# Sliding-window attention and a Sinkhorn-routed mixture of experts on one core: batch 7's blocks of x turned on TensorE, and four loads and starts moved

## The chip, the core and the metric

The kernel runs on one core of a Trainium2 chip. A core has a matrix engine (TensorE, PE in the profile), a vector engine (DVE), a scalar engine (ACT), GpSimd (POOL) and SyncE (SP), which here only issues transfers. Sixteen DMA engines carry the transfers of all queues. The time is that of one execution on the device, in microseconds (us); smaller is better. Three runs before the change gave a median of 1063.09 us (1062.86 to 1065.08).

## The reference

The inputs are q, k and v of 8 batches, 8 heads, 576 rows and 64 columns, and the weights of 8 experts. Attention sees at most 128 rows back and carries a bias that falls linearly with distance; its output, as 4608 rows of 512, is x. Every row then goes through every expert, and the experts' results are added with weights that come from eight rounds of normalising over rows and over columns.

```python
scores = where(0 <= rel < 128, q @ k.T / 8 - slope[h] * abs(rel), -1e9)
x = (softmax(scores) @ v).transpose(0, 2, 1, 3).reshape(4608, 512)
P = exp(x @ w_gate - max)
for _ in range(8):
    P /= P.sum(1, keepdims=True) + 1e-9
    P /= P.sum(0, keepdims=True) + 1e-9
    P *= 4608 / 8
for e in range(8):
    out += P[:, e:e+1] * (relu(x @ w1[e]) @ w2[e])
```

## The kernel before, in words

The order of the work is written out by hand: every engine carries out its instructions in the order in which the Python code emits them, and waits on semaphores where data or a buffer is not there yet. Tiles come from pools with a fixed number of buffers, so a load into a tile waits until the tile's previous user is done.

There are three stages.

**Attention, with experts 0 and 1 as filling.** A loop over `steps` runs through 8 batches, 5 blocks of rows (`kb`, four of 128 rows and a tail of 64) and 2 halves of the heads (`u`); inside a batch the half-blocks are numbered `at = 2 * kb + u`, 0 to 9. A half-block is a chain: scores on PE (L372, L379), exponentials on ACT (L390), a mask product on DVE (L403), the product with v on PE (`values`, L426), a reciprocal and a scaling on DVE (L436, L437). The result `xsb`, one block of x with rows in partitions, must be turned before the experts can use it (`turn_x`, L444). Batches below `XPE = 3` are turned on PE, with four transposes into PSUM (L454) and a copy by DVE (L462); the later batches are turned by a DMA that SP issues (L464). The turned x stays in `xT`. The four tails of 64 rows share blocks 32 to 35 in pairs, and the last of these, block 35, holds the tails of batches 6 and 7.

Between the parts of that chain the class `Filler` puts pieces of the first two experts on PE: `l1` is x times w1 (L102), `l2` is the second product (L115). A piece is allowed when its blocks of x are done (`filler.ready`) and its expert is in `filler.allowed`. Expert 0 is allowed from the start, expert 1 after half-block 1 of batch 1. Results go to a scratch tensor in HBM (`ysp`) by stores that SP issues (L484), those of the first four blocks of expert 0 in one store (L673). `gates` (L467, L470) multiplies the turned blocks by the gate weights; after the loop `gates(4 * B - 4, NBLK)` does blocks 28 to 35 in one go.

**Sinkhorn.** DVE does the eight rounds, with small products on PE, and `filler` puts batch 7's blocks of experts 0 and 1 between them.

**Experts 2 to 7.** Two thirds of the time; PE runs L829 and L884 without a break.

Two queues matter for the change. SP issues, in this order, the loads of batch 0 (L288, L334, L223), then q and k of batch 1 (`load_qk(1)`, L232), the tails of q and k of batch 1 (`load_tail(1)`, L223), the first block of v of batch 1 (`load_v(NKB)`, L334), and from the loop two more blocks of v, q and k of batch 2 after half-block 3 of batch 0, then v again. POOL casts each block of v to half precision (`cast_v`, L344) and issues the loads of the experts' weights, which convert to half precision on the way (`load_weights`, L86 and L88). It takes these in order too: the load of expert 1 stands behind the cast of v's block 0 of batch 1 (emitted after half-block 1 of batch 0).

Of the kernel before, what the change touches and what calls it, by code (L numbers as in the profile page):

```python
# [14 lines left out]
def kernel(  # L15
# [15 lines left out]
    B, H, S, Dh = q.shape  # L31
# [10 lines left out]
    NKB = 5  # L42
# [101 lines left out]
    XPE, YO = 3, 6  # L144
# [58 lines left out]
    if True:  # L203
# [16 lines left out]
        def load_tail(b):  # L220
            t32 = asb.tile([P, H, Dh], FP32, name=f"t32_{b}", tag="s32", bufs=5)
            for lo, src in ((0, q), (TL, k)):
                nc.sync.dma_start(  # L223
                    out=t32[lo : lo + TL], in_=src[b, :, SM:S, :].rearrange("h s d -> s h d")
                )
            tails[b] = t32

        def load_qk(b):
            q32 = per.tile([P, H, RI * Dh], FP32, name=f"q32_{b}", tag="a8", bufs=8)
            k32 = per.tile([P, H, RI * Dh], FP32, name=f"k32_{b}", tag="a8", bufs=8)  # L230
            for t, src in ((q32, q), (k32, k)):
                nc.sync.dma_start(  # L232
                    out=t, in_=src[b, :, 0:SM, :].rearrange("h (p i) d -> p h (i d)", i=RI)
                )
            raw[b] = (q32, k32)

        def cast_qk(b, j):

            if j == 0:
                c16s[b] = per.tile([P, 2, RI, H, Dh], FP16, name=f"c16_{b}", tag="a8", bufs=8)  # L240
            for n in (1, 0):
                src = raw[b][n][:, 2 * j : 2 * j + 2, :].rearrange("p h (i d) -> p i h d", i=RI)
                to = c16s[b][:, n, :, 2 * j : 2 * j + 2, :]
                if n == 0:
                    nc.vector.tensor_copy(out=to, in_=src)
                else:
                    nc.scalar.copy(out=to, in_=src)
            if j == NDT - 1:
                raw.pop(b)
# [80 lines left out]
        def load_v(m):  # L330
            b, kb = divmod(m, NKB)
            v32 = asb.tile([P, H, Dh], FP32, name=f"v32_{b}_{kb}", tag="s32", bufs=5)
            nk = P if kb < NKB - 1 else TL
            nc.sync.dma_start(  # L334
                out=v32[0:nk],
                in_=v[b, :, P * kb : P * kb + nk, :].rearrange("h s d -> s h d"),
            )
            v32s[b, kb] = v32

        def cast_v(m):  # L340
            b, kb = divmod(m, NKB)
            vt = asb.tile([P, H, Dh + 2], FP16, name=f"v_{b}_{kb}", tag="v", bufs=6)
            nk = P if kb < NKB - 1 else TL
            nc.gpsimd.tensor_copy(out=vt[0:nk, :, 0:Dh], in_=v32s.pop((b, kb))[0:nk])  # L344
            nc.gpsimd.memset(vt[:, :, Dh : Dh + 2], 1.0)
            vs[b, kb] = vt
# [7 lines left out]
        def sizes(kb):  # L354
            nk = P if kb < NKB - 1 else TL
            nn = 0 if kb == NKB - 1 else (P if kb < NKB - 2 else TL)
            return nk, nn
# [51 lines left out]
        def values(b, kb, u):  # L409
# [31 lines left out]
                op=ALU.mult,  # L441
            )

        def turn_x(b, kb):  # L444
            nk, _ = sizes(kb)
            if kb < NKB - 1:
                to = xT[:, 4 * b + kb]
            else:
                to = xT[:, 4 * B + b // 2, :, TL * (b % 2) : TL * (b % 2) + TL]
            xsb = xsbs.pop((b, kb))  # L450
            if b < XPE:
                ps = aps.tile([P, NDT, P], FP16, name=f"psX_{b}_{kb}", tag="pmm", bufs=4)
                for j in range(NDT):
                    nc.tensor.matmul(  # L454
                        out=ps[:, j, 0:nk],
                        lhsT=xsb[0:nk, 2 * j : 2 * j + 2, :],
                        rhs=ident[0:nk, 0:nk],
                        is_transpose=True,
                        start=(j == 0),
                        stop=(j == NDT - 1),  # L460
                    )
                nc.vector.tensor_copy(out=to, in_=ps[:, :, 0:nk])  # L462
            else:
                nc.sync.dma_start(out=to, in_=xsb[0:nk].rearrange("p h d -> p (h d)"), transpose=True)  # L464
# [36 lines left out]
        for n in range(2, len(spans)):  # L501
            order += [(0, n), (1, n - 2)]
        order += [(1, len(spans) - 2), (1, len(spans) - 1)]
        filler = Filler(
            (e, *spans[n], lambda e=e, n=n: unit_atoms(e, *spans[n], aps, ("pmm", "pmm"), (4, 4), keep))
            for e, n in order
        )
# [93 lines left out]
        nc.gpsimd.dma_start(out=wg_sb, in_=moe_w_gate.rearrange("(dt p) e -> p dt e", p=P))  # L601
        cast_v(3)
        cast_v(4)
        load_qk(1)
        load_tail(1)
        load_v(NKB)


        steps = [(b, kb, u) for b in range(B) for kb in range(NKB) for u in range(2)]
# [14 lines left out]
        for n, (b, kb, u) in enumerate(steps):  # L624
            nxt = steps[n + 1] if n + 1 < len(steps) else None
            at = 2 * kb + u
            left = ((8 if b < XPE else 10) - at) % 10 + 1
            budget = filler.backlog() / (11 if (b, at) == (XPE, 0) else left)
            if nxt:
                if nxt[0] < XPE and nxt[1:] == (RI - 2, 1):  # L630
                    turn_pe(nxt[0], 0, NDT)
                if nxt == (1, 0, 0):
                    cast_qk(1, 0)
                    cast_qk(1, 1)
                    for j in range(NDT):
                        turn_pe(1, 1, j)
                        turn_pe(1, 0, j)
                        if j < 2:
                            cast_qk(1, j + 2)
                        filler.fill(1.0)  # L640
                if n == 0:
                    scores(*nxt)
                elif nxt[2] == 0:
                    scores(*nxt)
                    scores(*nxt[:2], 1)
                exps(*nxt)
            got = filler.fill(1.0)
            if nxt:
                masks(*nxt)
            values(b, kb, u)  # L650
            if n > 0 and u == 0 and steps[n - 1][0] < XPE:
                turn_x(*steps[n - 1][:2])
            if u == 1 and n // 2 + NKB < B * NKB:
                cast_v(n // 2 + NKB)
            filler.fill(budget - got)
            if at == 0 and b > XPE:
                filler.ready = 4 * b
            if at < 8 and b < XPE:
                filler.ready = 4 * b + at // 2
            if at == 8 and b < XPE:  # L660
                filler.ready = 4 * b + 4
            if b >= XPE and u == 1:
                turn_x(b, kb)
            if u == 1:
                if kb == 1 and b > 0:
                    gates(4 * b - 4, 4 * b)
                if n // 2 + NKB + 1 < B * NKB:
                    load_v(n // 2 + NKB + 1)
            if b == 0 and at == 1:
                load_weights(1)  # L670
            if b == 1 and at == 1:
                filler.allowed.add(1)
                nc.sync.dma_start(out=ysp[0, 0:RI].rearrange("m p d -> p m d"), in_=first_y[0])  # L673
            if (b, at) == (0, 3):
                load_qk(2)
            if (b, at) == (0, 7):
                homes(1)
            if (b, at) == (1, 3):
                homes(2)
            if b == 1 and 3 <= at <= 6:  # L680
                cast_qk(2, at - 3)
            if b == 1 and 4 <= at <= 7:
                turn_pe(2, 1, at - 4)
                turn_pe(2, 0, at - 4)
            if 1 <= b < B - 2 and at == 3:
                load_qk(b + 2)
            if 1 <= b < B - 2 and at >= 8:
                cast_qk(b + 2, at - 8)
            if 2 <= b < B - 1:
                if at < 2:  # L690
                    cast_qk(b + 1, at + 2)
                if at == 1:
                    turn_qk(b + 1)
                    order_qk(b + 1, 1, range(NDT))
                if at == 5:
                    turn_tail(b + 1)
                if at in (6, 7):
                    order_qk(b + 1, 0, range(2 * at - 12, 2 * at - 10))
            if b < B - 1 and at == (1 if b > 1 else 5) and b:
                load_tail(b + 1)  # L700
            if 10 * b + at >= 66:
                i = 10 * b + at - 66
                if i % 8 == 0:
                    home_last(2 + i // 8)
                (load_w2 if i % 8 < 4 else load_w1)(2 + i // 8, i % 4, 4)
            if (b, at) == (7, 0):
                todo += sums_of(2, *extras(2))
            if b == 7 and at >= 5:
                some(1)
# [9 lines left out]
        F1_6 = lp.tile([P, NF2, HB], FP16, name="f1_6")  # L719
        todo += sums_of(4, *extras(4))  # L720

        filler.fill(4.4)
        gates(4 * B - 4, NBLK)
        filler.ready = NBLK

# [316 lines left out]
```

## Time and profile before

| | |
|---|---|
| median of three runs | 1063.09 us |
| the profiled execution | 1062.15 us |
| its span, first to last instruction | 1060.4 us |
| PE busy | 1031.0 us, 97% of the span |
| DVE, ACT, POOL busy | 629.8, 433.9 and 76.9 us |
| end of attention, start of L829 | about 284 us and 348 us |

The span is what the views of the profile cover; 1.75 us of the profiled execution lie around it. A line of a timeline gives the start and the length in us, the engine, the line of the kernel, the operation, what it writes and reads, and in square brackets how long the engine was idle before it and what ended the idle time. "L102 x8" are eight matmuls in one line. Busy tenths stand in 40 slices of 26.5 us.

### The profile page before, as it was taken

The page shows a single profiled execution, that of the slowest core. Times are in us where ns is not written, and L with a number is a line of the kernel's source. Part 1 is how long each engine was busy: PE and PEld are TensorE (multiplying, and loading weights), DVE is VectorE, ACT ScalarE, POOL GpSimd, SP SyncE. Part 2 cuts the span into 40 slices and gives each one's busy share as a digit, 9 for nine tenths or more (in the row PEclk, how much of TensorE's full clock was granted, in tenths as well). Part 3 has the DMA queues.
Part 4 walks back from the last instruction along what each step waited for, and adds up shares of the span by engine and source line. Part 5 has one row for each costly group of instructions (what it writes and reads, how often), then busy time and mean ns, then how long its engine had stood idle before and what let it go on. Part 6 is the DMA issues. An engine that isn't in the chain of part 4 may idle for free.

```text
span 1060.4 us, 21106 instructions
## 1 busy us (share of the span) xinstructions
PE 1031.0 (97%) x8986; PEld 802.0 (76%) x8986; DVE 629.8 (59%) x1166; ACT 433.9 (41%) x729; POOL 76.9 (7%) x139
## 2 busy tenths in 40 slices
PE   6799999999899999999999999999999999999998
PEld 4565444444444888888888888888888888888887
DVE  4565665555488565655655655655655655555555
ACT  6565554555233333333333333333333333333332
POOL 2122032334000000000000000000000000000000
PEclk9999999999999999999999999999999999999999
DMA  9996598969992501201211211211220220220240
GB/s 227 250 221 165 103 213 206 195 156 167 193 202 72 120 21 50 71 24 48 70 28 43 70 41 31 70 24 48 71 63 8 71 68 4 70 70 2 71 90 20
DMA packets 168574, 99.14 MB, mean 94 GB/s; under 512 B 87424, under 2 KB 159904, under 8 KB 168480
## 3 DMA queue, kind: packets, MB, share of 16 engines
q1 hardware_dynamic: 153744, 79.80, 29.9%
q0 software_dynamic: 14304, 17.84, 10.3%
q8 instruction: 70, 1.15, 0.4%
q14 instruction: 24, 0.20, 0.1%
q10 hardware_dynamic: 432, 0.16, 0.1%
HBM read 87.74 MB, written 19.02 MB: 101 GB/s over the span
## 4 chain that ended last, share of the span: by engine, by line
PE 90%; DMA 6%; DVE 1%; SPq 1%; ACT 1%; issue 0%; POOL 0%; DVEq 0%
PE psh L829 35%; PE psS_m L884 31%; PE psh L102 11%; PE psy L115 10%; DMA xT<-xsb 2%; DMA v<-in_v_dram 2%; PE psN L426 1%; DMA w1t<-in_moe_w_dram 1%; PE psS L372 1%; SPq L223 1%; DMA pbc<-ptd 1%; DVE yo L496 1%; SPq L334 0%; PE psy L949 0%; DMA k<-in_k_dram 0%
## 5 line engine op out<-in xcount | busy, mean ns | idle before, releaser
L836 ACT ACTIVATE hs<-psh 128x512 f16<-128x512 f32 x432 | 257.9, 597 | 453.4 <-PE psh L829 372.6
L829 PE MATMUL psh<-aux,w1l 128*128 128x256 f16 x2880 | 372.6, 273 | 0.4 <-DVE aux L813 0.4
L829 PEld LDWEIGHTS <-w1l 128*128 128x128 f16 x2880 | 281.7, 98 | 33.5 <-issue 0.6
L884 PEld LDWEIGHTS <-hs 128*128 128x128 f16 x2568 | 251.2, 98 | 29.1
L841 DVE TENSOR_TENSOR hs<-hs 128x1024 f16<-128x1024 f16 x107 | 74.0, 691 | 274.5 <-ACT hs L836 274.5
L884 PE MATMUL psS_m<-w2l,hs 128*128 128x256 f16 x1440 | 186.6, 273 | 0.0
L102 PE MATMUL psh<-xT,w1t 128*128 128x512 f16 (+1 forms) x640 | 144.1, 364 | 7.9 <-DMA w1t<-in_moe_w_dram 3.0
L115 PE MATMUL psy<-w2t,hT 128*128 128x512 f16 x576 | 133.8, 379 | 2.3 <-DMA w2t<-in_moe_w_dram 1.6
L813 DVE TENSOR_TENSOR aux<-xT,pbc 128x1024 f16<-128x1024 f16 x108 | 131.3, 1216 | 2.7 <-DMA pbc<-ptd 2.7
L109 ACT ACTIVATE hT<-psh 128x512 f16<-128x512 f32 (+1 forms) x160 | 87.3, 556 | 106.0 <-PE psh L102 105.2
L102 PEld LDWEIGHTS <-w1t 128*128 128x128 f16 x640 | 58.4, 100 | 58.4 <-issue 8.0
L115 PEld LDWEIGHTS <-hT 128*128 128x128 f16 x576 | 53.7, 98 | 63.6 <-issue 3.8
L390 ACT ACTIVATE pt<-psS 128x1024 f16<-128x1024 f32 (+2 forms) x80 | 67.4, 852 | 42.1 <-PE psS L372 34.4
L930 DVE TENSOR_TENSOR acc<-acc,psS_m 128x256 f32<-128x256 f32 (+1 forms) x162 | 74.3, 504 | 12.4 <-PE psS_m L884 11.1
L496 DVE CAST yo<-psy 128x512 f16<-128x512 f32 x68 | 46.8, 690 | 58.5 <-PE psy L115 54.7
L829 PE MATMUL psh<-aux,w1t 128*128 128x256 f16 x576 | 74.6, 273 | 0.0
L884 PE MATMUL psS_m<-more,hs 128*128 128x256 f16 x576 | 74.6, 273 | 0.0
L403 DVE TENSOR_TENSOR pt<-pt,mask 128x1024 f16<-128x1024 f16 (+2 forms) x80 | 50.2, 628 | 39.9 <-ACT pt L390 39.6
L844 DVE TENSOR_TENSOR hs<-hs 128x1024 f16<-128x1024 f16 x107 | 73.2, 684 | 0.0
L829 PEld LDWEIGHTS <-w1t 128*128 128x128 f16 x576 | 56.4, 98 | 6.5
L532 POOL DMA_DIRECT2D w2t<-in_moe_w_dram x2 | 1.8, 880 | 705.4 <-PE psS_m L884 670.0
L426 PEld LDWEIGHTS <-pt 128*128 128x128 f16 (+2 forms) x576 | 29.0, 102 | 23.6 <-issue 6.1
(83 smaller groups left out, 648.4 us busy)
## 6 DMA issues: line engine op xcount, KB each, us to landing
pbc<-ptd SPq DMA_DIRECT2D x108, 128.0 KB, 4.5
y<-ysp SPq DMA_DIRECT2D x36, 256.0 KB, 4.7
ysp<-yo SPq DMA_DIRECT2D x68, 128.0 KB, 3.3
v<-in_v_dram SPq DMA_DIRECT2D x32, 256.0 KB, 4.1
out_dram<-acc SPq DMA_DIRECT2D x31, 256.0 KB, 2.5
q<-in_q_dram SPq DMA_DIRECT2D x7, 1024.0 KB, 6.6
k<-in_k_dram SPq DMA_DIRECT2D x7, 1024.0 KB, 9.0
w2t<-in_moe_w_dram POOLq DMA_DIRECT2D x4, 1024.0 KB, 14.9
```

Of the source, the lines that this page charges most:

```text
L102: nc.tensor.matmul(out=ps[:, 0:nt], lhsT=w1ts[e][:, dt, P * ft : P * ft + P], rhs=xT[:, b0 : b0 + nb, dt, :], start=(dt == 0), stop=(dt == ...
L109: nc.scalar.activation(out=st["hT"][:, ft, 0:nt], in_=ps[:, 0:nt], func=AF.Relu)
L115: nc.tensor.matmul(out=ps, lhsT=st["hT"][:, ft, P * ms : P * ms + P], rhs=w2ts[e][:, ft, :], start=(ft == 0), stop=(ft == NFT - 1),)
L390: nc.scalar.activation(out=pt[0:nk, :, 0 : nk + nn], in_=ps[0:nk, :, :, 0 : nk + nn].rearrange("p a y n -> p (a y) n"), func=AF.Exp, scale ...
L496: nc.vector.tensor_copy(out=yo, in_=ps)
L813: nc.vector.tensor_tensor(out=xs(n).rearrange("p (d b t) -> p d b t", d=NDT, b=2), in0=xT[:, 2 * g : 2 * g + 2].rearrange("p b d t -> p d ...
L829: nc.tensor.matmul(out=ps[:, f, :], lhsT=W1L[e][:, dt, P * ft : P * ft + P], rhs=xs(n)[:, HB * dt : HB * dt + HB], start=(dt == 0), stop=( ...
L836: nc.scalar.activation(out=h[n][:, 2 * i : 2 * i + 2, :], in_=ps, func=AF.Relu)
L841: nc.vector.tensor_tensor(out=t[:, NFT : NFT + NF2, :], in0=a[:, 0:NF2, :], in1=a[:, NF2:NFT, :], op=ALU.add)
L844: nc.vector.tensor_tensor(out=t[:, NFT + NF2 : 2 * NFT, :].rearrange("p f n -> p (f n)").rearrange("p (f t) -> p f t", t=P), in0=a[:, :, P ...
L884: nc.tensor.matmul(out=Ms[g, bank][:, half, :], lhsT=left(n, m, f), rhs=W2L[e][RIGHT[m]][:, f, :], start=(e == 2 and f == 0 and half == 0) ...
L930: nc.vector.tensor_tensor(out=a, in0=a, in1=p2, op=op)
```

## The change

Four things change.

1. `by_pe(b)` takes the place of `b < XPE`: the five blocks of batch 7 are now turned on PE as well, by four transposes and a DVE copy each. Blocks 0 to 3 are turned one half-block later than the DMA was, after the first `values` of the next block; the tail is turned after the loop, inside what was `filler.fill(4.4)`. In the instruction order that results, two pieces of L115 stand ahead of this last turn and none behind it; then come the gates.
2. q and k of batch 1 are asked for after the tails and the first block of v of batch 1, and no longer ahead of them.
3. The load of expert 1's weights moves from after half-block 1 to after half-block 7 of batch 0. On POOL it now stands behind the casts of v's blocks 0, 1, 2 and 3 of batch 1, and ahead of the cast of block 4.
4. Expert 1 is allowed, and the first store of `ysp` issued, after half-block 2 of batch 1, and no longer after half-block 1. The first product of expert 1 on PE comes behind one more `values`, one more turn and one more pair of scores than before.

```diff
+        def by_pe(b):
+            return b < XPE or b == B - 1
+
         def turn_x(b, kb):
...
-            if b < XPE:
+            if by_pe(b):
                 ps = aps.tile([P, NDT, P], FP16, name=f"psX_{b}_{kb}", tag="pmm", bufs=4)
...
-        load_qk(1)
         load_tail(1)
         load_v(NKB)
+        load_qk(1)
...
-            if n > 0 and u == 0 and steps[n - 1][0] < XPE:
+            if n > 0 and u == 0 and by_pe(steps[n - 1][0]):
                 turn_x(*steps[n - 1][:2])
...
-            if b >= XPE and u == 1:
+            if u == 1 and not by_pe(b):
                 turn_x(b, kb)
...
-            if b == 0 and at == 1:
+            if b == 0 and at == 7:
                 load_weights(1)
-            if b == 1 and at == 1:
+            if b == 1 and at == 2:
                 filler.allowed.add(1)
                 nc.sync.dma_start(out=ysp[0, 0:RI].rearrange("m p d -> p m d"), in_=first_y[0])
...
-        filler.fill(4.4)
+        filler.fill(1.0)
+        turn_x(B - 1, NKB - 1)
+        filler.fill(2.6)
         gates(4 * B - 4, NBLK)
```

## The prediction, written before the result was known

> **What bounds the kernel now.** I read the page first, then PE's waits, then PE's timeline at the two places that the change touches, then POOL's timeline and the transfers issued around them.
>
> ```profile
> PE 1031.0 (97%) x8986; PEld 802.0 (76%) x8986; DVE 629.8 (59%) x1166; ACT 433.9 (41%) x729; POOL 76.9 (7%) x139
> PE   6799999999899999999999999999999999999998
> ```
>
> PE is busy for 97%; 29 us are left, most of them in the first two slices (53 us) and a little in the eleventh. So only two things can pay: fewer waits of PE in those places, or less work on PE. Anything that another engine does beside PE is free. PE's waits by name:
>
> ```profile
> PE psT L311 <- ACT c L247: 7.0, 3, 5.3
> PE psG L470 <- DMA xT<-xsb: 3.7, 2, 3.0
> PE psh L102 <- DMA w1t<-in_moe_w_dram: 3.0, 1, 3.0
> PE psy L115 <- DMA w2t<-in_moe_w_dram: 1.6, 1, 1.6
> ```
>
> The 5.3 us are the start and don't change. The second row is the end of attention, the third the first product of expert 1. PE's timeline at both:
>
> ```profile
> 48.47 0.30 PE L426 MATMUL psN<-v,pt 128*128 128x65 f16 x4 [0.60 <-DVE pt L403]
> 51.73 1.05 PE L102 MATMUL psh<-xT,w1t 128*128 128x256 f16 x8 [2.96 <-DMA w1t<-in_moe_w_dram]
> ...
> 285.02 0.56 PE L470 MATMUL psG<-wg_sb,xT 128*128 128x8 f16 x16 [0.74 <-DMA xT<-xsb]
> 288.57 0.26 PE L470 MATMUL psG<-wg_sb,xT 128*128 128x8 f16 x4 [2.99 <-DMA xT<-xsb]
> 288.68 1.86 PE L102 MATMUL psh<-xT,w1t 128*128 128x512 f16 x4
> ```
>
> Four matmuls of that form elsewhere take 0.97 us, here 1.86. The busy time by stretches says why: the last column but two is the granted clock.
>
> ```profile
> 285.30:288.72 3.42, 0.43 (x17) 0.34 (x14) 0.69 (x1) 0.00 (x0) 0.00 (x0) 1.00 1.15 213
> 288.72:292.13 3.41, 3.41 (x13) 1.11 (x10) 0.96 (x3) 0.60 (x1) 2.64 (x4) 0.50 0.52 81
> ...
> 49.80:53.20 3.40, 1.47 (x20) 1.32 (x21) 1.21 (x4) 0.76 (x2) 0.00 (x0) 1.00 1.18 210
> 53.20:56.60 3.40, 3.40 (x41) 2.67 (x39) 1.66 (x6) 2.37 (x7) 0.00 (x0) 1.00 1.21 198
> ```
>
> After a stretch with 0.43 us of work PE ran 3.41 us at half clock, which costs 1.7 us; the wait of 2.96 us at 51.73, in a stretch with 1.47 us of work, cost nothing more. POOL issues expert 1's weights behind the cast of a block of v:
>
> ```profile
> 37.56 0.61 POOL L344 CAST v<-v 128x512 f16<-128x512 f32 x1 [12.73 <-DMA v<-in_v_dram]
> 38.11 0.11 POOL L345 MEMSET v<- 128x16 f16 x1
> 38.16 0.74 POOL L86 DMA_DIRECT2D w1t<-in_moe_w_dram  x1
> ...
> 59.09 0.61 POOL L344 CAST v<-v 128x512 f16<-128x512 f32 x1 [17.95 <-DMA v<-in_v_dram]
> ```
>
> The last row is the cast of block 3 of batch 1, behind which the load stands in the changed kernel.
>
> **The change, part by part.**
>
> *q and k of batch 1 behind tails and v.* By the list of transfers k was issued at 14.61 and took 20.8 us (35.4); the second tail landed at 27.90 + 8.6 = 36.5, v at 29.75 + 7.8 = 37.5. The DMA engines' share is 1.07 to 1.19 in every stretch of 10 us from 10 to 60, so the order changes and not the sum: k takes the last place, 37.5, some 2.1 us later. SP is not the limit: the tail's issue, which sat 12.0 us behind q and k, goes ahead, q and k sit there in its place. The cast of k (ACT, 35.51) and the first turn on PE (36.18) follow to 38.3. The 1.6 us wait for expert 0's w2 at 30.63 may shrink, but then PE waits for k instead. So PE gets to the first product of expert 1 about 2 us later than at 48.77, at 50.9.
>
> *Expert 1 one half-block later.* Ahead of its first product now stand a `values` and a turn (52.62 to 53.25) and a pair of scores (54.22 to 54.76): 0.63 + 0.54 = 1.17 us of work that PE does before the wait and saves behind it. With one wait for a mask (0.60, as at 48.47) PE stands there at 52.7.
>
> *Expert 1's weights behind block 3's cast.* Block 3 is issued behind q and k of batch 2. q: issued at 36.16, 8.0 us, 44.2; the set of bytes ahead is the same as before. k: 16.8 us before, with expert 1's weights beside it; with those gone it follows q by 2.9 (97.25 + 8.8 against 96.56 + 6.6) to 3.8 us (61.38 + 10.6 against 60.19 + 8.0), so 47.1 to 48.0. v follows by 0.93 (29.75 + 7.8, 31.97 + 6.5, 35.01 + 4.4 land 0.93 apart): 48.0 to 48.9, I take 48.5. Cast and memset 0.6: the issue comes at 49.1, where it was 38.16. A load of this size took 8.7 us almost alone (312.6), 9.3 with a thin stream of v beside it (12.32), 13.5 beside q and k (38.16). Two blocks of v, the first store of y, one more v and then q and k of batch 3 will be beside it; the store waits for a DVE copy at about 50, which holds up the rest. I take 9.3: landing 58.4, with 57.3 and 63.0 as the ends. The first product then starts at 58.4 and not at 51.73, with 1.17 us already done: +5.5 us (+4.4 with 8.7 and the earliest v, +10.1 with 13.5 and the latest). Part 2's 2.1 us lie inside this wait and cost nothing. w2 was issued 0.73 behind w1 and landed at 58.7, 7 us after it; in the changed kernel some 65.5, and it is wanted after ten pieces of L102 (5 us) and 4 us of attention, 67.4.
>
> *The clock behind that wait.* PE stands from 52.7 to 58.4, 5.7 us. Ends: 0 (the 2.96 us row) and 1.7 (the 2.99 us row). A wait twice as long, with nearly nothing in it, is nearest to the second: +1.7. The Trainium skill, "TensorE: Matmul & The Clock Gate", section "HAM oscillation — how this bites in real kernels", says 'The abstract rule is "no PE-idle gaps >~3.4µs."' and ties it to fixed windows of 3.4 us that run on their own. By that rule 5.7 us nearly surely empties a window, and the two rows differ only by where the wait fell; with the term at 0 the sum below would be 1.7 less.
>
> *Batch 7 turned on PE.* Gone: waits 0.74 + 2.99 and the half clock 1.7, together 5.4 us. New on PE: five turns; one takes 0.37 us from its start to the next instruction (52.88 to 53.25), 1.85 in all. DVE gets five copies of 0.41 us (L462 at 53.62), 2.05 us, hidden: it idles 41% and PE runs on pieces of L102 and L115; uncovered it would be 2.05. The last copy stands behind one cast of y (0.69 us) and takes 0.28; the gates of blocks 28 to 34 take about 1 us meanwhile, so the four matmuls of block 35 wait 0 to 0.3. SP loses five DMA transposes; the stores of y behind them leave earlier, so DVE's 2.63 us wait for a y buffer at 286.24 goes too. What is late next is DVE's reduction chain, which had PE wait 0.58 at 331.58 and keeps its distance. Net -3.6; the ends are -4.4 (turns overlapped, 0.2 each) and -2.1 (three waits of 0.5 for a copy, as at 75.42).
>
> *Sum.* +5.5 + 1.7 - 3.6 = +3.6 us. The profiled execution took 1062.15 (span 1060.4 and 1.75 around it), so 1065.75 on it; the median of the runs is 0.94 higher, so 1066.7. A measurement of this kernel tells about 0.2%, 2.1 us.
>
> **The rivals.** Let s be the start of expert 1's first product; the early change is s - 51.73 - 1.17 and a clock term of 0 to 1.7.
>
> - *Faster: the weights arrive in time.* With no q and k beside it, the load may need far less than 8.7 us. The change pays measurably if s is below 54.4 (54.4 - 52.9 - 3.6 = -2.1, no clock term). That asks for a transfer of 5.3 us from 49.1, or a block 3 that lands 4 us earlier; at s = 53.5 the time is 1060.1. For it: v's block 3 took 20.7 us before, so the old figures are crowded ones. Against it: no row has under 8.7. The Trainium skill, "DMA: Bandwidth & Descriptors", section "Anatomy of one DMA — SWDGE (gpsimd) path", fits 2.0 us plus bytes over 436e3 per us; an estimate from it is 4.4 us for the megabyte written, 6.8 for the two read. That would make s 53.5 or 55.9, and the time 1060.1 or 1062.5; the trace's rows disagree with it by 1.9 us at least, and they decide.
> - *The same.* s near 56.5 to 57.5 and little or no half clock: +3.6 to +4.6 against -3.6, 1063.1 to 1064.1. Speaks for it: 8.7 us and the early v give 57.3, 1063.9 if the clock holds.
> - *Slower still: crowded weights.* q and k of batch 3 come in beside w1 as at 38.16: s = 63.0, +10.1 + 1.7 - 3.6 = +8.2, 1071.3.
> - *The turns don't pay.* If the last DVE copy waits behind a y buffer as the cast at 286.24 did, the 2.99 us and the half clock stay: +5.5 + 1.7 + 1.85 - 0.74 = +8.3, 1071.4. Against it: nothing holds the stores any more.
>
> **How the numbers follow.** Forecast 0.46, in time 0.16, the same 0.22, crowded 0.10, turns 0.06. Slower is 0.46 + 0.10 + 0.06 = 0.62, the same 0.22, faster 0.16. The predicted time is 1066.7. Its own range, from s = 57.0 with half of the clock term (+4.1 + 0.85 - 3.6) to s = 60 with all of it (+7.1 + 1.7 - 3.6), is 1064.4 to 1068.3. The range of 8 in 10 is 1061.0 to 1071.0: below lies most of the faster case, above it part of the last two.
>
> **What would show it.** Right: POOL's L86 for expert 1 at 48 to 50; the first L102 from it with an idle time of 5 to 7 us ended by w1t, and half clock behind it; the turn of q and k at about 38; psG L470 without a wait for xT; L102 after the gates at 0.97 us for four. The prediction is wrong if w1t lands before 55, if PE's idle there is below 3 us, or if the gates still wait. It would also be wrong if k of batch 1 landed several us later than 37.5, since that shifts PE's arrival towards 58 and turns the wait into a delay of the same size without the half clock.

## The result, and the profile after

| | before | changed |
|---|---|---|
| median | 1063.21 us | 1065.08 us |
| runs | 22, 1059.7 to 1065.9 | 22, 1064.1 to 1069.1 |
| profiled execution (span) | 1062.15 us (1060.4) | 1065.72 us (1063.9) |
| ratio to before | 1 | 1.0019, 95% interval 1.0011 to 1.0028 |

The changed kernel is slower by 1.9 us, where +3.6 us was forecast; by the interval the change is 1.2 to 3.0 us. It lies at the edge of the 0.2% that a measurement of this kernel tells, on the slower side. The two profiled executions differ by 3.57 us.

From the page of the changed kernel, busy time of the engines and the slices of PE and of its granted clock:

```profile
PE 1035.9 (97%) x9006; PEld 805.9 (76%) x9006; DVE 632.0 (59%) x1171; ACT 435.0 (41%) x729; POOL 76.4 (7%) x139
...
PE   6889999999999999999999999999999999999998
...
PEclk9889999999999999999999999999999999999999
```

PE has 20 matmuls more, which are the five turns, and 4.9 us more of busy time. The dip in the eleventh slice (265 to 291 us) is gone. The second slice is fuller, with part of its work at half clock. PE's waits, by name (total us, times, longest):

```profile
PE psT L311 <- ACT c L247: 10.2, 3, 5.3
PE psh L102 <- DMA w1t<-in_moe_w_dram: 3.7, 2, 2.6
PE psN L426 <- DVE pt L403: 3.2, 4, 1.0
```

The gates (psG) have no row any more. The first row has grown from 7.0 to 10.2 us: that is the later k of batch 1. POOL's timeline, where expert 1's weights are asked for, and then PE's timeline at the turn of that k, at expert 1's first product and at the end of attention:

```profile
48.48 0.61 POOL L344 CAST v<-v 128x512 f16<-128x512 f32 x1 [7.92 <-DMA v<-in_v_dram]
49.03 0.11 POOL L345 MEMSET v<- 128x16 f16 x1
49.08 0.74 POOL L86 DMA_DIRECT2D w1t<-in_moe_w_dram  x1
```

```profile
38.64 1.03 PE L311 MATMUL psT<-ident,c 128*128 128x128 f16 x8 [3.74 <-ACT c L247]
39.92 1.87 PE L102 MATMUL psh<-xT,w1t 128*128 128x256 f16 x8 [0.25 <-ACT kN L326]
...
58.05 1.89 PE L102 MATMUL psh<-xT,w1t 128*128 128x256 f16 x8 [2.57 <-DMA w1t<-in_moe_w_dram]
...
292.89 0.29 PE L457 MATMUL psX<-ident,xsb 64*128 64x64 f16 x4
293.11 1.08 PE L473 MATMUL psG<-wg_sb,xT 128*128 128x8 f16 x32
294.05 1.02 PE L102 MATMUL psh<-xT,w1t 128*128 128x512 f16 x4
```

All 32 matmuls of the gates are one line without idle time, and four matmuls of L102 behind them take 1.02 us where they took 1.86. Eight matmuls of L102 at 58.05, however, take 1.89 us (1.05 in the kernel before). The busy time by stretches says why, as before by the granted clock, the last column but two:

```profile
37.00:40.50 3.50, 1.61 (x11) 1.28 (x12) 0.79 (x2) 2.24 (x4) 1.27 (x4) 0.50 1.00 234
40.50:44.00 3.50, 3.50 (x26) 2.84 (x24) 1.36 (x3) 2.26 (x5) 0.06 (x2) 0.56 1.09 361
55.50:59.00 3.50, 0.95 (x5) 0.71 (x6) 1.26 (x3) 0.82 (x1) 0.00 (x0) 0.75 1.09 209
59.00:62.50 3.50, 3.50 (x24) 2.58 (x23) 0.61 (x2) 1.53 (x4) 0.66 (x2) 0.50 1.19 223
```

Half clock set in during both waits, and lasted from 36.74 to 43.57 and from 57.22 to 64.04, two stretches of 3.41 us each time. The first cost nothing in this profile, since it only made PE come to the weights later (its wait there is 2.57 and not 5.7 us). Of the second PE worked through 5.99 us, which loses 3.0.

**Where the time went, in the two profiles.** Expert 1's first product starts 5.15 us later, less the work done ahead of it (58.05 - 51.73 - 1.17). Half clock behind it takes 3.0. The five turns take some 0.23 us each (285.06 to 285.30 is one), 1.15 in all. That is 9.3 us; the gates start at 293.11 and not at 283.84, 9.27 later. From the start of the gates to L102 behind them it was 4.84 us and is now 0.94, which gives back 3.90, and the half clock behind it is gone, 1.7. What is left is 3.67; the spans differ by 3.5.

### The profile page after: what moved, and what is told of

The parts are those of the page before. It is cut to its first block, busy times and chain, and to the rows that moved or that the text cites. A ratio compares the mean times of both kernels' runs of the same rounds, so it can differ in the third digit from the quotient of the medians.

```text
span 1063.9 us, 21146 instructions
## 1 busy us (share of the span) xinstructions
PE 1035.9 (97%) x9006; PEld 805.9 (76%) x9006; DVE 632.0 (59%) x1171; ACT 435.0 (41%) x729; POOL 76.4 (7%) x139
## 3 DMA queue, kind: packets, MB, share of 16 engines
q0 software_dynamic: 14304, 17.84, 10.2%
q8 instruction: 70, 1.15, 0.5%
## 4 chain that ended last, share of the span: by engine, by line
PE 89%; DMA 6%; SPq 1%; DVE 1%; ACT 1%; issue 0%; POOL 0%; ACTq 0%; POOLq 0%; DVEq 0%
PE psh L834 35%; PE psS_m L889 30%; PE psh L102 10%; PE psy L115 10%; DMA v<-in_v_dram 3%; PE psN L426 1%; DMA xT<-xsb 1%; PE psS L372 1%; DMA w1t<-in_moe_w_dram 1%; DMA pbc<-ptd 1%; DVE yo L499 0%; ACT pt L390 0%; SPq L334 0%; SPq L223 0%; DMA ident<-ident_c 0%
## 5 line engine op out<-in xcount | busy, mean ns | idle before, releaser
L102 PE MATMUL psh<-xT,w1t 128*128 128x512 f16 (+1 forms) x640 | 146.0, 368 | 7.6 <-DMA w1t<-in_moe_w_dram 3.7
L115 PE MATMUL psy<-w2t,hT 128*128 128x512 f16 x576 | 133.8, 379 | 0.6 <-DMA w2t<-in_moe_w_dram 0.4
L102 PEld LDWEIGHTS <-w1t 128*128 128x128 f16 x640 | 59.7, 102 | 58.7 <-issue 6.8
L115 PEld LDWEIGHTS <-hT 128*128 128x128 f16 x576 | 53.7, 98 | 62.1 <-issue 1.2
L935 DVE TENSOR_TENSOR acc<-acc,psS_m 128x256 f32<-128x256 f32 (+1 forms) x162 | 74.3, 504 | 12.4 <-PE psS_m L889 11.1
```

What stands on the lines that cost most here:

```text
L102: nc.tensor.matmul(out=ps[:, 0:nt], lhsT=w1ts[e][:, dt, P * ft : P * ft + P], rhs=xT[:, b0 : b0 + nb, dt, :], start=(dt == 0), stop=(dt == ...
L115: nc.tensor.matmul(out=ps, lhsT=st["hT"][:, ft, P * ms : P * ms + P], rhs=w2ts[e][:, ft, :], start=(ft == 0), stop=(ft == NFT - 1),)
L935: nc.vector.tensor_tensor(out=a, in0=a, in1=p2, op=op)
```

## The experiments

Every ratio is to the kernel before, run beside it on the same chip (its median was 1062.3 to 1063.0 us each time). Four questions: do the parts cost what the sum said; is it the place of the weights; what did the order of q and k do; and does the clock behind the waits count.

### One part at a time

The turns of batch 7 alone, with all loads as before:

```diff
+        def by_pe(b):
+            return b < XPE or b == B - 1
...
-        filler.fill(4.4)
+        filler.fill(1.0)
+        turn_x(B - 1, NKB - 1)
+        filler.fill(2.6)
```

> Only batch 7's turns on TensorE, all loads and starts as before. Theory A (the two waits for xT of 0.74 and 2.99 us and the half clock of 1.7 us behind them go, five turns at 0.37 us come): 3.6 us faster than before, some 1059.5 us, the gates without a wait, and the wait for expert 1's w1 of about 3 us still there. Rival B (the turns do not pay, because the last copy stands behind a cast that waits): 1 to 2 us slower than before, a wait of 2 to 3 us stays at the gates. Rival C (PE's own work for the turns costs twice what I took, 0.75 us each): 1.7 us faster.

Measured: 1059.21 us, ratio 0.9957 (0.9942 to 0.9972), 3.7 us faster, as theory A had it. PE's timeline of this kernel:

```profile
51.77 1.89 PE L102 MATMUL psh<-xT,w1t 128*128 128x256 f16 x8 [3.22 <-DMA w1t<-in_moe_w_dram]
...
286.59 1.09 PE L473 MATMUL psG<-wg_sb,xT 128*128 128x8 f16 x32
287.54 1.02 PE L102 MATMUL psh<-xT,w1t 128*128 128x512 f16 x4
```

Neither the wait of the gates nor the half clock behind them came back elsewhere. The first line is of use below: the wait for the weights is as long as in the kernel before (3.22 to 2.96 us, at nearly the same time), yet here eight matmuls take 1.89 us and not 1.05.

The loads alone, that is parts 2 to 4 without the turns:

```diff
-        load_qk(1)
         load_tail(1)
         load_v(NKB)
+        load_qk(1)
...
-            if b == 0 and at == 1:
+            if b == 0 and at == 7:
                 load_weights(1)
-            if b == 1 and at == 1:
+            if b == 1 and at == 2:
```

> Only the three moves of loads and starts, x of batch 7 turned by DMA as before. Theory A (expert 1's w1 lands at 58, which sets PE back by 5.2 us, with half clock of 1.7 to 3 us behind the waits; the half clock at the end of attention stays): 5 to 8 us slower than before, 1068 to 1071 us. Rival B (the moves cost nothing by themselves, what the changed kernel lost is the work of the turns): within 1.5 us of before.

Measured: 1068.78 us, ratio 1.0056 (1.0035 to 1.0076), 5.9 us slower, as theory A had it. PE's timeline:

```profile
59.29 1.89 PE L102 MATMUL psh<-xT,w1t 128*128 128x256 f16 x8 [5.00 <-DMA w1t<-in_moe_w_dram]
...
293.06 0.56 PE L470 MATMUL psG<-wg_sb,xT 128*128 128x8 f16 x16 [0.26 <-DMA xT<-xsb]
295.97 0.27 PE L470 MATMUL psG<-wg_sb,xT 128*128 128x8 f16 x4 [2.35 <-DMA xT<-xsb]
296.10 1.87 PE L102 MATMUL psh<-xT,w1t 128*128 128x512 f16 x4
```

The gates wait and the half clock follows, as before the change. -3.7 and +5.9 are +2.2, and both together measured +1.9: as far as the intervals tell, the two halves add up.

### The place of the weights

The changed kernel with the weights issued after half-block 5, and after half-block 1, where it stood before (`at == 1` in the same line):

```diff
-            if b == 0 and at == 7:
+            if b == 0 and at == 5:
```

> The changed kernel with expert 1's weights asked for after half-block 5 of batch 0, behind the cast of v's block 2. Theory A (place on POOL and company set the landing: issue at 40.5, beside q and k of batch 2, 13.5 us, landing 54): expert 1's first product at about 55.5, where TensorE arrives anyway, wait under 1 us, and 2 to 3.5 us faster than the changed kernel, 1061.5 to 1063 us. Rival B (the order of the loads does not matter, since the sum of the bytes is the same): 1065 us.

> The changed kernel with expert 1's weights asked for after half-block 1 of batch 0 again, behind the cast of v's block 0, which is early here. Theory A (the issue comes at 32.5, beside q and k of batch 1; the wait moves from the weights to k): k's cast at 41 to 44 and not at 37.9, no wait for w1, expert 1's first product at 58 to 61: 1064 to 1067 us. Rival B (the earlier the weights, the better): 1061 us or less, k no later than 39.

Measured: half-block 5, 1058.87 us, ratio 0.9971 (0.9957 to 0.9985); half-block 1, 1060.71 us, ratio 0.9977 (0.9969 to 0.9986). POOL's timeline of the first:

```profile
39.55 0.74 POOL L86 DMA_DIRECT2D w1t<-in_moe_w_dram  x1
```

and of the second:

```profile
32.81 0.74 POOL L86 DMA_DIRECT2D w1t<-in_moe_w_dram  x1
...
47.61 0.61 POOL L344 CAST v<-v 128x512 f16<-128x512 f32 x1 [13.17 <-DMA v<-in_v_dram]
51.12 0.61 POOL L344 CAST v<-v 128x512 f16<-128x512 f32 x1 [2.85 <-DMA v<-in_v_dram]
```

After half-block 5 POOL waits for block 2 of v only, whose cast ends at 39.5, and not for block 3, which in the changed kernel lands at 48.5. The weights leave 9.5 us earlier, take 11.7 us and land at 51.2, and PE, which gets to their product at 53.58, has no wait for them. This edit alone turns a loss of 1.9 us into a gain of 3.5 beside its kernel before. The place, then, carries the loss, as the theory had it, and the gain was larger than I expected. After half-block 1 I expected the weights to hold up q and k of batch 1; they did not. The turn of that k came at 39.52, 0.9 later than in the changed kernel. What came later were the casts of blocks 1 and 2 of v (at 39.07 and 39.89 in the changed kernel, 8.5 and 11.2 us earlier), whose loads SP issued from 30.77 to 35.2, beside the weights, and which took 17.7 us; the kernel is still faster than the one before. The rival held there (k's cast at 38.85, and 1060.71 us). Whether half-block 5 is better than 1 the two intervals do not tell.

The same place with q and k of batch 1 asked for first, as before the change:

```diff
+        load_qk(1)
         load_tail(1)
         load_v(NKB)
-        load_qk(1)
...
-            if b == 0 and at == 7:
+            if b == 0 and at == 5:
```

> The changed kernel with q and k of batch 1 first again, and expert 1's weights asked for after half-block 5 of batch 0. Theory A (the place of the weights decides, the order of q and k is worth 2 us at most): POOL issues w1 at 41 to 42, beside q and k of batch 2, landing 53 to 55, first product there, TensorE waiting 1.5 to 4 us for it; 1058.5 to 1062 us, some 7 to 10 us faster than the same kernel with the weights after half-block 7. Rival B (the order of q and k is the cost): 1065 us or more.

Measured: 1059.19 us, ratio 0.9958 (0.9943 to 0.9973). POOL's and PE's timeline of it:

```profile
41.94 0.74 POOL L86 DMA_DIRECT2D w1t<-in_moe_w_dram  x1
```

```profile
53.73 1.89 PE L102 MATMUL psh<-xT,w1t 128*128 128x256 f16 x8 [0.82 <-DMA w1t<-in_moe_w_dram]
```

The wait for the weights is 0.82 us, shorter than the 1.5 to 4 expected, and the time is as theory A had it. The kernel that differs from this one by the place alone is the next one, and it is 9.7 us slower.

### The order of q and k

The prediction said that the order of q and k (part 2) costs nothing, because the weights' wait hides it. So undoing it alone should change nothing:

```diff
+        load_qk(1)
         load_tail(1)
         load_v(NKB)
-        load_qk(1)
```

> The changed kernel with q and k of batch 1 asked for ahead of tails and v again. Theory A (the later k is hidden inside the wait for expert 1's w1, which is set by its place on POOL behind v's block 3): the same time as the changed kernel within 1.5 us (one half clock less at 39 us can be had), the wait for k 0.9 us instead of 3.7, the wait for w1 longer by about 3 to 4 us, POOL's issue of w1 still at 49. Rival B (the later k is what costs): 3 us or more faster than the changed kernel, 1062 us or less.

Measured: 1068.87 us, ratio 1.0055 (1.0037 to 1.0074), against 1.0019 (1.0011 to 1.0028) for the changed kernel. Both theories missed: with the late weights, the order that the change brought is worth 3.8 us. I first suspected q and k of batch 3, which here go out at 50.8 and 52.1 us beside the weights, and moved them from half-block 3 to half-block 6 of batch 1:

```diff
-            if 1 <= b < B - 2 and at == 3:
+            if 1 <= b < B - 2 and at == (6 if b == 1 else 3):
```

> The kernel with q and k of batch 1 first (1068.9 us), and q and k of batch 3 asked for after half-block 6 of batch 1 and no longer after half-block 3. Theory A (that kernel is slower than the changed one because its store of y goes out 2.4 us earlier, and q and k of batch 3 behind it come in beside expert 1's w1, which took 10.3 us and not 8.9): with these later the load takes 8.7 to 9.3 us, first product at 57.5 to 58.8, and the time falls by 1.5 to 4 us to that of the changed kernel, 1065 to 1067 us. Rival B (the difference is w2 of expert 0 or the half clock, not the company of w1): 1068 us or more.

Measured: 1068.54 us, ratio 1.0058 (1.0044 to 1.0072). PE's timeline:

```profile
60.57 1.89 PE L102 MATMUL psh<-xT,w1t 128*128 128x256 f16 x8 [8.97 <-DMA w1t<-in_moe_w_dram]
```

The time is the one that the rival named, but the reason for it is not: the weights still took 10.9 us, so it is their transfer that is long, and q and k of batch 3 alone do not make it so. To see the two orders beside each other on one chip, three more profiles: the order undone, the changed kernel, the order undone.

> The kernel of e3_qk_first, looked at once more: its profile (1065.9 us) was the fastest of its eight runs, which had a median of 1068.9. Theory A (the load of w1 takes longer in the usual run, 11 to 13.5 us, since the store of y, v and q and k of batch 3 are out earlier beside it): w1 lands at 60.5 to 63. Rival B (only the half clock differs): w1 lands at 59.9 as in the first look, and more of the half clock lies behind it.

> The changed kernel, looked at once more. Theory A: w1 issued at 48.5 to 49.5, 8.9 to 10.5 us to its landing, first product at 58 to 59.5; half clock behind at least one of the two waits, at another place than in the first look, since its windows run on their own; 1064 to 1067 us.

> The kernel of e3_qk_first a third time, for the same question as the second: is it w1's landing that makes its usual run 3 us longer than the one first looked at (Theory A: 60.5 us or later), or the half clock alone (Rival B: landing at 59.9 or before).

Measured, one execution each: 1068.01, 1064.86 and 1066.98 us. PE's timeline at the first product of expert 1, of these three kernels in that order:

```profile
60.49 1.89 PE L102 MATMUL psh<-xT,w1t 128*128 128x256 f16 x8 [9.20 <-DMA w1t<-in_moe_w_dram]
```

```profile
57.44 1.89 PE L102 MATMUL psh<-xT,w1t 128*128 128x256 f16 x8 [3.07 <-DMA w1t<-in_moe_w_dram]
```

```profile
60.90 1.89 PE L102 MATMUL psh<-xT,w1t 128*128 128x256 f16 x8 [9.03 <-DMA w1t<-in_moe_w_dram]
```

The three profiles with the order undone start it at 59.87, 60.49 and 60.90, the two of the changed kernel at 58.05 and 57.44: 2.7 us apart on average. In the same profiles the weights were asked for at about the same time (48.5 to 49.5 against 48.2 and 49.1) and took 10.3, 11.9 and 11.6 us against 8.9 and 9.2. So the later start is the transfer of the weights, as theory A had it for the second and third profile with the order undone (60.5 or later); the changed kernel's second came half a microsecond earlier than I expected. What lay beside it shows in the DMA queues (packets, MB, share of 16 engines; q0 is POOL's queue, q1 SP's), in the changed kernel from 50.2 to 57.4 us:

```profile
q0 software_dynamic: 617, 1.12, 90.9%
q1 hardware_dynamic: 225, 0.23, 11.3%
```

and in the third of these, with the order undone, from 51.3 to 60.9 us:

```profile
q0 software_dynamic: 689, 1.21, 72.6%
q1 hardware_dynamic: 1623, 0.85, 34.5%
```

The eight profiles with the weights after half-block 7, with q1 counted from about 2 us after the issue of the weights to their landing, and the issue of the first store of `ysp` given against that of the weights:

| kernel | first store of `ysp` | packets of q1 | share of q1 | first packet of q0 | weights' transfer |
|---|---|---|---|---|---|
| changed | 3.0 us after | 181 | 9.4% | 1.25 us | 8.9 us |
| changed, again | 2.6 us after | 225 | 11.3% | 1.25 us | 9.2 us |
| loads alone | 2.2 us after | 376 | 16.4% | 1.25 us | 10.5 us |
| changed, PE kept busy (below) | 0.4 us after | 722 | 24.4% | 2.0 us | 10.5 us |
| order undone | 0.2 us after | 703 | 25.8% | 2.5 us | 10.3 us |
| order undone, q and k of batch 3 late | 1.6 us before | 1537 | 24.2% | 2.75 us | 10.9 us |
| order undone, third | 1.7 us before | 1623 | 34.5% | 3.0 us | 11.6 us |
| order undone, again | 1.1 us before | 1590 | 32.7% | 2.75 us | 11.9 us |

The column before the last is the time from the issue of the weights to the first packet that POOL's queue moves, in steps of 0.25 us. By and large, the more SP's queue has on the engines, the longer the weights take. With the order undone 1.25 to 1.75 us more than in the changed kernel pass before their first packet. In the last three rows SP's queue takes three quarters or more of the engines' time until then. In "loads alone" the first packet is as early as in the changed kernel, and the transfer is 1.3 to 1.6 us longer all the same, so the start is not all of it.

The store waits for results of PE's first pieces, and SP's list stands behind it. A late k of batch 1 delays PE, the store, and all that SP issues behind it; k early, or PE kept busy, brings them out beside the weights. This chain is read from the eight profiles; no run moved the store by itself. The Trainium skill, "DMA: Bandwidth & Descriptors", section "Queues, rings and completion order", has each engine take turns between the queues that have work for it, a packet at a time. The table agrees in direction; the single turns are not seen in it, and by themselves they would not keep the weights' packets out for 2.5 to 3 us. Which of SP's transfers it is (the store, blocks of v, the tails of batch 3) no run told apart.

The later landing is not all that differs in these five profiles. The half clock set in before the weights landed, so a part of it lies behind the first product, and half of that part is lost. When the gates of blocks 28 to 35 start follows from both:

| kernel | first product | half clock until | lost behind it | gates start | gates less product and loss |
|---|---|---|---|---|---|
| changed | 58.05 | 64.04 | 3.0 us | 293.11 | 232.1 us |
| changed, again | 57.44 | 62.89 | 2.7 us | 292.19 | 232.0 us |
| order undone | 59.87 | 62.51 | 1.3 us | 293.11 | 231.9 us |
| order undone, again | 60.49 | 66.50 | 3.0 us | 295.39 | 231.9 us |
| order undone, third | 60.90 | 63.61 | 1.4 us | 294.19 | 231.9 us |

With the order undone the product comes 2.7 us later, but on average 1.0 us less is lost behind it, and the gates start 1.6 us later. The profiled executions differ by nearly the same: 1066.97 against 1065.29 us on average. The 3.8 us of the medians are more than these five profiles show, and the difference between the two stays open.

### The clock behind the waits

If the half clock behind the two waits costs time, PE must be given work in them. Dummy matmuls of 512 columns, whose result nobody reads, 14 ahead of the turn of k and 16 ahead of expert 1's first product, in the changed kernel:

```diff
+        def busy(n, tag):
+            ps = aps.tile([P, GT], FP32, name=f"busy_{tag}", tag="pmm", bufs=4)
+            for i in range(n):
+                nc.tensor.matmul(
+                    out=ps, lhsT=ident, rhs=xT[:, 0, :, :], start=(i == 0), stop=(i == n - 1)
+                )
...
+                    busy(14, 0)
...
+            if (b, at) == (1, 3):
+                busy(16, 1)
```

> The changed kernel with 14 matmuls of 512 columns ahead of the turn of q and k of batch 1, and 16 ahead of expert 1's first product; nobody reads what they write. They put 3.0 and 3.5 us of work on TensorE into its two waits. Theory A (the half clock behind the waits is a cost of its own, on top of the late weights): no half clock between 36 and 64 us, expert 1's first product at 58 as before, and 1.5 to 3 us faster than the changed kernel, 1062 to 1063.5 us. Rival B (the weights' landing alone sets the time, half clock behind it is made up elsewhere): 1065 us. Rival C (the added work reaches past the landing): slower than the changed kernel by up to 2 us.

Measured: 1063.17 us, ratio 1.0009 (0.9997 to 1.0021). PE's timeline and the busy time by stretches:

```profile
52.87 5.31 PE L447 MATMUL busy<-xT,ident 128*128 128x512 f16 x16
...
59.27 1.05 PE L102 MATMUL psh<-xT,w1t 128*128 128x256 f16 x8 [1.09 <-DMA w1t<-in_moe_w_dram]
```

```profile
53.00:56.40 3.40, 3.40 (x9) 1.22 (x8) 1.22 (x3) 0.78 (x1) 0.00 (x0) 0.50 1.11 232
56.40:60.00 3.60, 2.51 (x16) 1.26 (x14) 0.00 (x0) 0.03 (x1) 0.00 (x0) 1.00 1.17 199
```

The half clock falls on the dummy work, and the first product runs at full clock, 1.05 us. In this profile the weights came 1.2 us later than in the changed kernel's (59.27), and still the gates started 2.0 us earlier (291.14), 231.9 us behind a product with nothing lost behind it. So in the profile half clock is a cost of its own, as theory A had it, though one stretch of it stayed between 52.96 and 56.37. The mean granted clock of the whole run was 0.995 to 0.998 in all eleven runs, where the 22 of the changed kernel have 0.991 to 0.995. The median is 1.9 us below the changed kernel's, by the two ratios 1.1 us, but the intervals overlap, and so the size of the gain in time is not settled.

### A version that beats both

The turns, and expert 1 allowed one half-block later, with the loads as before the change:

```diff
+        def by_pe(b):
+            return b < XPE or b == B - 1
...
-            if b == 1 and at == 1:
+            if b == 1 and at == 2:
                 filler.allowed.add(1)
```

> The turns, and expert 1 allowed one half-block later, with the order of q and k and the place of the load of expert 1's weights as before. Theory A (w1 lands at 51.7 as before and PE does 1.17 us of attention ahead of the wait): the wait for w1 falls from 2.96 to about 1.2 to 1.8 us, and the time is 1.2 us below that of the turns alone, some 4.8 us below before, 1058.3 us. Rival B (the half-block without filling waits for its own chain as long as it saves): the same as the turns alone, 1059.5 us.

Measured: 1058.04 us, ratio 0.9956 (0.9942 to 0.9971). PE's timeline:

```profile
51.26 1.89 PE L102 MATMUL psh<-xT,w1t 128*128 128x256 f16 x8 [0.26 <-DMA w1t<-in_moe_w_dram]
```

With the weights asked for at 38.27 PE's wait falls from 3.22 us with the turns alone to 0.26, more than the 1.17 us of work that now stand ahead of it: a second wait for a mask (1.01 us) stands there too, and the product starts 0.5 us earlier. The median is the lowest of all, but 1.2 us below the turns alone is less than these intervals tell. The medians by the place of the weights and the order of q and k, all with the turns and expert 1 allowed after half-block 2 (they come from different chips, on which the kernel before had 1062.3 to 1063.2):

| weights after half-block | 1 | 5 | 7 |
|---|---|---|---|
| q and k of batch 1 first | 1058.04 | 1059.19 | 1068.87 |
| behind tails and v | 1060.71 | 1058.87 | 1065.08 |

The order that the change brought gains only where the weights are late; with the weights early its median is 2.7 us the higher one, though the two intervals just touch.

## Why the prediction was right, and where it was not

- *Direction and the two main causes* held. Slower was given 0.62, and the time lies in the range. The loss is the weights behind block 3's cast, which the run with the weights after half-block 5 shows, the gain the turns; the loads and the turns were timed by themselves (+5.9 and -3.7).
- *Expert 1's weights.* The issue was forecast at 49.1 and came at 49.08; the transfer at 9.3 us, and took 8.9 and 9.2; the first product at 58.4, and started at 58.05 and 57.44. k of batch 1 was to land at 37.5 and its turn to come at 38.3: 37.9 and 38.64. w2 landed at 66.7 (forecast 65.5), and no wait of PE for a w2 is longer than 0.4 us.
- *The length of the wait* failed: 2.57 us in the first profile and 3.07 in the second, not 5 to 7, and an idle time below 3 us was one of the prediction's own signs that it is wrong. I had taken PE's arrival at 52.7 from work at full clock and one wait for a mask. During the wait for the later k of batch 1 the clock had gone to half, from 36.74 to 43.57, two waits for masks came (0.60 and 1.02 us), and PE was there at 55.5. As I had argued of the 2.1 us of part 2, this lies inside the wait; it does not move the start of the product.
- *The clock behind it* was mis-sized: +1.7 forecast, 3.0 by the trace, since half clock lasted from 57.22 to 64.04, two stretches of 3.41 us and not one. That half clock would come was right, the reason only in part: I had argued from a wait of 5.7 us with nearly nothing in it, but the wait was 2.57 us, and the stretch ahead of the half clock (53.81 to 57.22) held 1.32 us of work.
- *The turns of batch 7.* Net -3.6 forecast, -3.7 measured by the medians. Inside it one turn was mis-sized: 0.37 us forecast, about 0.23 measured, so five cost 1.15 and not 1.85. The copies did hide, and DVE's last copy stood behind one cast of y as foreseen.
- *The sum* came out well in part by luck. By the profiles the later product cost 5.15 us where 5.5 were forecast, the clock 3.0 for 1.7, and the turns with the waits and the half clock that they removed -4.45 for -3.6. The errors of -0.35, +1.3 and -0.85 cancel, so that +3.57 stands beside +3.6.
- *The crowded weights* (13.5 us) and *the turns that don't pay* did not come; nor did weights in time. The estimate from the Trainium skill, "DMA: Bandwidth & Descriptors", section "Anatomy of one DMA — SWDGE (gpsimd) path", 4.4 to 6.8 us, had no support here either: the shortest transfer of these weights took 8.9.
- *The step from the profiled execution to the median* is where +3.6 became +1.9. I added 0.94 us, the distance of the kernel before from its own median. In the end that distance was 1.06 for the kernel before, and the changed kernel's profiled execution lies 0.64 above its median, not below it. By the profiles alone the change is +3.57, by the medians +1.87. The turns were met by their median, so the miss lies in the loads, +5.9 measured for +7.2, and the interval of that run (about +3.7 to +8.1) holds both. What differs from run to run can be named in part: in the profile of the kernel before the wait of 2.96 us left no half clock, with the turns alone one of 3.22 us did. The kernel before so pays in some runs a part of what the changed one always pays, and its profile was one in which it did not pay. The granted clock of each run, averaged over the run, bears this out. The profile of the kernel before has 0.997; of the 60 runs of that kernel beside the experiments, the 15 with 0.997 or more have a median of 1061.5 us, the 24 with 0.994 or less one of 1063.2. The 22 runs of the changed kernel have 0.991 to 0.995, and their times do not go with it. That this makes up the whole 1.7 us is not shown.
- *"Part 2 costs nothing"* was right as a cost with the weights this late, but it saw only half of what the order does. The order of q and k has a second effect which I had not looked for: it changes what SP has on the DMA engines thirty microseconds later, beside the weights. Undone in the changed kernel it made it 3.8 us slower. That this goes by way of PE and the store is read from the profiles, not tested by itself.

## What to carry to other kernels

Before moving the issue of a large load on a queue that works in order, write down what the instruction ahead of it waits for: here one cast more (that of block 3, against block 2) cost 9.5 us of issue, and the load, which landed 2.3 us before its product in that version, did not have so much to give. A wait of a few microseconds on PE has a second price, in half clock behind it, which one profile can show and the next one not; count it by its chance and not by one profile's row. And where two changes that have nothing in common arrive together, time them apart: here one was worth 3.7 us and the other cost 5.9.

## What the runs showed of the hardware that I had not expected

- Waits of nearly the same length at nearly the same time (2.96 us at 51.73 and 3.22 us at 51.77) had full clock behind them in one profile and 1.89 us for eight matmuls in the other. The Trainium skill, "TensorE: Matmul & The Clock Gate", section "Part 1: The HAM clock gate (the "warmup" mystery)", says that its window of 3.4 us runs freely and doesn't reset when a kernel starts. These two rows agree: in the kernel before the two stretches of 3.41 us on which the wait lies held 1.80 and 1.47 us of work, with the turns alone the stretch from 46.86 held 1.08, and half clock followed. A wait of 3.22 us, shorter than a stretch, was enough for it.
- A stretch at half clock can be followed by a second one though PE works in it. In the one from 57.22 PE was busy from 58.05 on, 2.58 of 3.41 us, and half clock went on to 64.04; in the kernel before, a stretch at full clock with 1.47 us of work was not followed by half clock. Stretches of 3.41 us, counted from a change of the clock, give a limit for the first kind: in all fourteen profiles, up to 350 us, a stretch at half clock with up to 2.59 us of PE work was followed by another, one with 2.64 or more by full clock. So a product that had started 0.1 us earlier than 58.05 might have been spared the second stretch. At full clock the rows show no such line: between 15 and 72 us, 1.33 us or less always led to half clock, 1.48 to 1.79 did in several profiles, and 1.47, 1.74 and 1.83 in others did not.
- A load asked for earlier lands earlier by nearly as much, and what it pushes back is what is asked for beside and behind it: asked for at 32.81, 39.55, 41.94 and 49.08 us, the weights took 11.1, 11.7, 11.7 and 8.9 us. I had expected the first of these to hold up q and k, which SP had issued before; k came 0.9 us later.
- An order of loads can act through the other queue much later: q and k put ahead of the tails and v at 15 us, and not behind them, made the weights' transfer at 50 us 1.1 to 3.0 us longer; the profiles suggest that it goes by way of PE, a store and SP's list.
